# Spreading one kernel's dense matmuls anew over its attention units, and a different bank for the first product of its tail

## Chip, cores, metric

The kernel runs on one core of a Trainium2 chip. The metric is the device time of one execution in microseconds (us). The kernel before takes 654.57 us (median of 3 runs, 654.51 to 654.58). In the profile, TensorE appears as PE (matmuls) and PEld (weight loads), VectorE as DVE, ScalarE as ACT, GpSimd as POOL, and SyncE, which issues the DMAs, as SP.

## The reference

The reference has two branches on the layer norm of the same input and a residual. Branch B is a two-layer MLP over the tokens. It fills the first 387 us and the change does not touch it. Branch A is attention in 4 segments of 512 tokens with 32 heads of 32, plus a memory carried from segment to segment:

```python
phi = lambda t: jnp.where(t > 0, t + 1.0, jnp.exp(t))
for s in range(N):                                     # N = 4 segments
    qs, ks, vs = q[:, :, s], k[:, :, s], v[:, :, s]
    logits = einsum('bhqd,bhkd->bhqk', qs, ks) * scale + mask
    a_dot = einsum('bhqk,bhkd->bhqd', softmax(logits), vs)
    a_mem = einsum('bhld,bhde->bhle', phi(qs), M) / (... + 1e-06)
    outs.append(g * a_mem + (1.0 - g) * a_dot)
    M = M + einsum('bhld,bhle->bhde', phi(ks), vs)     # and z likewise
return stack(outs) @ wo
...
return x + A(xn, wq, wk, wv, wo, beta) + B(xn, w1, b1, w2, b2)
```

## The kernel before

Branch A runs as 32 "units": 4 segments of 8 groups of 4 heads. In each unit PE does two kinds of work.

- The unit's own chain. The logits of the unit are computed in two or three steps ("logits"). ScalarE takes their exp (1.88 us each), GpSimd masks them (the "select"), and one unit later PE multiplies them by v in three parts ("the weighing"). VectorE then copies ("ost"), scales ("srec"), multiplies ("prod") and adds ("o_s") the result, and a transposing DMA puts it in oT.
- Dense filler. These are jobs of 8 matmuls of 512 columns that make q, k and v of later units and the output product with wo. They are cut into pieces and put between the steps of the chain, so that PE has work while the other engines follow. Each job adds up its 8 matmuls in one of the eight banks (0 to 7) that the kernel keeps for PE's results (ps_all in the profile), and another engine then copies or adds the sum out of the bank (the job's "drain").

All of it is scheduled by hand. These are the parts that matter:

```python
def dense(self, n, side=True):            # n more matmuls of the queued jobs
    while n > 0 and self.jobs:
        job = self.jobs[0]
        at, b, reads, mm, end, on_dve = job
        stops = self.stops[on_dve] if side else ()
        if b is None:                     # a new job takes bank 6 or 7, in turn
            b = job[1] = 6 + self.turn
            self.turn ^= 1
        ...
        with fw.group(reads=reads(), writes=[self.R_bank[b]]):
            for i in range(at, stop):
                mm(b, i)
        ...
        if stop == 8:
            end(b)                        # the drain of the bank
            self.jobs.popleft()
        elif self.side and stop in stops:
            self.side.popleft()()         # one of VectorE's side tasks is queued here

# drains: q_job  ScalarE copy to qT           (line 1252 in the profile)
#         k_job  VectorE copy to kT           (line 1261)
#         v_job  ScalarE copy to vA, some on VectorE   (line 1292)
#         wo_job VectorE add to fin           (line 1306)

def unit_jobs(self, u):
    jobs = [self.wo_job(*self.wo_jobs.popleft())] if 10 <= u < self.QUOTA_FROM else []
    m = u // 4 + 1
    if m < 2 * N_SEG:
        jobs.append(self.v_job(m, u % 4))
    if u + 2 < N_UNIT:
        jobs.append(self.q_job(u + 2))
        if u + 2 < N_UNIT // 2:
            jobs.append(self.k_job(u + 2))
        ...
    if u >= self.QUOTA_FROM:              # 18: from here a unit gets a quota
        quota = self.QUOTA[u % 2] if u + 1 < N_UNIT else 100
        quota -= 8 * len(jobs) + sum(8 - j[0] for j in self.jobs)
        while quota > 0 and self.wo_jobs:
            jobs.append(self.wo_job(*self.wo_jobs.popleft()))
            quota -= 8
        self.left = max(-quota, 0)        # carried into the next unit
    return jobs

# one unit, in the order in which PE gets its work
    cuts = self.cut(total, (0, 4, 2, 4, 1, 13, 8) if even else (7, 3, 2, 4, 1, 15))
    self.dense(cuts[0]);  self.logits(u, 0)
    self.dense(cuts[1]);  self.weigh(u - 1, 0)         # bank 4
    self.dense(cuts[2], False);  self.weigh(u - 1, 1)  # bank 5
    self.dense(cuts[3], False);  self.weigh(u - 1, 2)  # bank 4 again
    # queue the side tasks for VectorE: srec; phi of q; prod; o_s; phi of k
    self.dense(cuts[4]);  self.logits(u, 1)
    if even:
        self.dense(cuts[5]);  self.logits(u, 2)
    self.dense(...)                                    # the rest of the unit's share

# the logits of all steps use banks 0 to 3; each step ends so:
    fw.op("act", exp of the four banks into pT)        # line 1363, 1.88 us
    fw.op("pool", affine_select of pT)                 # line 1367
    self.late_exps()                                   # exp of q and k for phi, line 1218

# tail: the last 8 products of 8 matmuls; product n goes to bank
    (0, 1, 2, 3, 6, 7, 5, 4)[n]
```

A dense job can start only when the job two before it has been drained from its bank. And the drain is queued on ScalarE or VectorE at the moment at which the job's last matmul is issued, so the point of the unit at which a job ends decides which work lies ahead of its drain.

## Time and profile before

| | before |
|---|---|
| time, median of 3 runs | 654.57 us |
| span of the profiled run | 652.2 us |
| PE busy | 646.7 us, 99% |
| VectorE, ScalarE, GpSimd busy | 67%, 43%, 24% |
| matmuls | 4611 |

The page of the kernel before: its first line, the first line of the busy times (each engine with its share of the span and its instructions), and the chain that ended last.

```profile
span 652.2 us, 11204 instructions
...
PE 646.7 (99%) x4611; PEld 303.1 (46%) x4611; DVE 439.9 (67%) x829; ACT 281.5 (43%) x305; POOL 154.9 (24%) x181
...
PE 90%; DVE 4%; DMA 2%; ACT 1%; POOL 1%; issue 1%; DVEq 0%
```

PE is the bound almost everywhere (busy 646.7 of 652.2 us). In the trace two dense matmuls in a row start 216 ns apart. I take that pace as given. So only stalls in PE's stream can be won.

The next view gives busy time per stretch for units 10 and 11 together and for units 14 and 15 together. The columns are the stretch in us, its length, then busy time and instructions of each engine, granted clock, DMA share, and GB/s.

```profile
core 0: us, PE busy (x) PEld busy (x) DVE busy (x) ACT busy (x) POOL busy (x), PEclk, DMA share, GB/s
461.77:481.01 19.24, 19.11 (x193) 9.35 (x194) 17.35 (x35) 13.42 (x14) 7.46 (x10) 1.00 0.51 121
...
499.94:515.61 15.67, 15.65 (x178) 7.75 (x178) 14.81 (x32) 12.45 (x11) 6.70 (x9) 1.00 0.55 138
```

VectorE is busy 17.35 of 19.24 us and 14.81 of 15.67 us there, so these units have little of VectorE to spare.

The last view of the kernel before is the timeline, at unit 28 and in the tail. Its columns are start in us, duration (with "x" more than one instruction), engine, line, operation, output<-input, shapes and count. In brackets stand the idle time of the engine just before, and what ended it.

```profile
604.73 1.22 DVE L1460 TENSOR_TENSOR prod<-ost,srec 128x1024 bf16<-128x1024 bf16 x1
...
605.10 2.11 POOL L1367 TENSOR_SCALAR_AFFINE_SELECT pT<-pT 128x512 bf16<-128x512 bf16 x2 [2.54 <-ACT pT L1363]
...
605.50 0.82 PE L199 MATMUL ps_all<-wo,oT 128*128 128x512 bf16 x3
...
606.58 0.25 PE L199 MATMUL ps_all<-vA,pT 128*128 128x33 bf16 x4 [0.26 <-POOL pT L1367]
...
607.56 0.64 POOL L1367 TENSOR_SCALAR_AFFINE_SELECT pT<-pT 128x512 bf16<-128x512 bf16 x1 [0.35 <-ACT pT L1363]
...
633.89 2.75 PE L199 MATMUL ps_all<-wo,oT 128*128 128x512 bf16 x12 [0.24 <-ACT pT L1363]
...
640.46 1.84 PEld L199 LDWEIGHTS ps_all<-wo,oT 128*128 128x128 bf16 x10 [0.49 <-DMA oT<-o_s]
```

At 606.58 the weighing waits 0.26 us for a select. The two selects that start at 605.10 take 2.11 us together, against 0.64 us for the single one at 607.56. At 633.89 the first tail product waits 0.24 us, because its bank 0 is still being read by an exp. At 640.46 a weight load waits for the transposing DMA of oT. (The idle times in brackets count from the modelled end of the last matmul. The delay against the usual distance from start to start is some 0.16 us longer: 0.42 us for this weighing, 0.41 us for this product.)

### The profile page before, as it was taken

Reading aid. Unit: us, or ns where it says so; the run is one execution under the profiler, and the core shown is the slowest. Engines: PE = TensorE matmul, PEld = TensorE weight load, DVE = VectorE, ACT = ScalarE, POOL = GpSimd, SP = SyncE. Lnnn points to the kernel's source line nnn. Section 1 sums busy time; section 2 is a strip of 40 time slices with the busy share of each in tenths; the row PEclk is TensorE's granted clock in tenths of the full one; section 3 lists DMA queues with packets and bytes.
Section 4 is the critical chain, followed back from the end, with each engine's and each line's share of the span. In section 5 each row is a group of like instructions: output and inputs, shape, how many; then the busy total and the mean of one; then the engine's idle time right before and its main releaser. Section 6 shows DMA issues by size and latency. Waiting matters only on the chain.

```text
span 652.2 us, 11204 instructions
## 1 busy us (share of the span) xinstructions
PE 646.7 (99%) x4611; PEld 303.1 (46%) x4611; DVE 439.9 (67%) x829; ACT 281.5 (43%) x305; POOL 154.9 (24%) x181
## 2 busy tenths in 40 slices
PE   9999999999999999999999999999999999999998
PEld 3444444444444444444444444444545444454444
DVE  6975775665655673745637325767898988887895
ACT  7542232232210000111101047778767788888760
POOL 2500000000011220120201203434333445544450
PEclk9999999999999999999999999999999999999999
DMA  8804242242498937629263956979644576355424
GB/s 300 217 0 130 65 116 79 65 124 70 129 265 216 231 96 210 171 87 258 66 193 116 257 136 156 190 182 227 124 120 109 152 164 144 90 115 123 114 81 138
DMA packets 190123, 95.00 MB, mean 146 GB/s; under 512 B 108664, under 2 KB 176248, under 8 KB 190072
## 3 DMA queue, kind: packets, MB, share of 16 engines
q1 hardware_dynamic: 189928, 94.25, 56.9%
q8 instruction: 36, 0.59, 0.4%
q14 instruction: 15, 0.12, 0.1%
q10 hardware_dynamic: 144, 0.03, 0.0%
HBM read 69.23 MB, written 11.53 MB: 124 GB/s over the span
## 4 chain that ended last, share of the span: by engine, by line
PE 90%; DVE 4%; DMA 2%; ACT 1%; POOL 1%; issue 1%; DVEq 0%
PE ps_all L199 90%; ACT pT L1363 1%; DMA w2s<-in_B_w_dram 1%; POOL pT L1367 1%; DVE fin L1617 1%; DVE ln_st L590 1%; DVE sum L651 0%; DVE prod L1460 0%; DMA xin<-in_A_x_dram 0%; DVE h L630 0%; POOL ln_rs L614 0%; DVE mtmp L1229 0%; DVE mtmp L1227 0%; DVE ost L1414 0%; DVE part L692 0%
## 5 line engine op out<-in xcount | busy, mean ns | idle before, releaser
L1363 ACT ACTIVATE pT<-ps_all 128x2048 bf16<-128x2048 f32 x80 | 150.2, 1877 | 47.2 <-PE ps_all L199 46.8
L1367 POOL TENSOR_SCALAR_AFFINE_SELECT pT<-pT 128x512 bf16<-128x512 bf16 x128 | 106.3, 847 | 160.9 <-ACT pT L1363 160.9
L692 DVE TENSOR_TENSOR part<-ps_all,part 128x512 f32<-128x512 f32 x84 | 57.7, 690 | 108.9 <-PE ps_all L199 88.2
L1078 POOL TENSOR_TENSOR part<-part,stg 128x512 f32<-128x512 f32 x24 | 33.0, 1402 | 285.0 <-DVE part L692 268.1
L749 ACT ACTIVATE g<-part,b1c 128x512 f16<-128x512 f32 x36 | 26.0, 722 | 99.0 <-DVE part L692 99.0
L199 PE MATMUL ps_all<-wv,xnT 128*128 128x512 bf16 x256 | 68.2, 380 | 0.2
L199 PE MATMUL ps_all<-xnT,wq 128*128 128x512 bf16 x256 | 65.6, 380 | 0.0
L199 PE MATMUL ps_all<-wo,oT 128*128 128x512 bf16 (+2 forms) x272 | 64.3, 367 | 0.2 <-ACT pT L1363 0.2
L1414 DVE CAST ost<-ps_all 128x396 bf16<-128x396 f32 (+2 forms) x96 | 44.3, 473 | 27.3 <-PE ps_all L199 26.6
L697 ACT ACTIVATE part<-ps_all 128x512 f32<-128x512 f32 x24 | 14.0, 596 | 101.4 <-PE ps_all L199 67.1
L199 PEld LDWEIGHTS ps_all<-vA,pT 128*128 128x128 bf16 x1280 | 45.5, 96 | 21.5 <-DVE ost L1414 3.3
L199 PE MATMUL ps_all<-g,sum 128*128 128x512 f16 x224 | 51.0, 379 | 0.0
L199 PE MATMUL ps_all<-g,w2s 128*128 128x512 f16 x224 | 51.0, 379 | 0.0
L199 PE MATMUL ps_all<-gT,sum 128*128 128x512 f16 x224 | 50.3, 379 | 0.1
L199 PE MATMUL ps_all<-vA,pT 128*128 128x33 bf16 x1280 | 48.5, 178 | 0.7 <-POOL pT L1367 0.6
L199 PE MATMUL ps_all<-h,sum 128*128 128x512 f16 x192 | 45.2, 379 | 0.0
L199 PE MATMUL ps_all<-h,w1s 128*128 128x512 f16 x192 | 44.9, 379 | 0.0
L199 PE MATMUL ps_all<-hT,sum 128*128 128x512 f16 x192 | 43.6, 379 | 0.0
L199 PEld LDWEIGHTS ps_all<-wo,oT 128*128 128x128 bf16 x272 | 23.8, 97 | 27.1 <-issue 4.9
L1460 DVE TENSOR_TENSOR prod<-ost,srec 128x1024 bf16<-128x1024 bf16 x24 | 35.1, 1461 | 0.0
L199 PEld LDWEIGHTS ps_all<-gT,sum 128*128 128x128 f16 x224 | 21.8, 98 | 26.8 <-DVE gT L666 0.6
L199 PEld LDWEIGHTS ps_all<-g,w2s 128*128 128x128 bf16 x224 | 21.9, 98 | 26.4
(118 smaller groups left out, 862.2 us busy)
## 6 DMA issues: line engine op xcount, KB each, us to landing
w2s<-in_B_w_dram SPq DMA_DIRECT2D x8, 1792.0 KB, 9.5
w1s<-in_B_w_dram SPq DMA_DIRECT2D x12, 1024.0 KB, 5.6
wq<-in_A_wq_dram SPq DMA_DIRECT2D x32, 256.0 KB, 3.4
xs<-in_A_x_dram SPq DMA_DIRECT2D x24, 256.0 KB, 3.4
stg<-in_A_x_dram SPq DMA_DIRECT2D x16, 256.0 KB, 2.8
out_dram<-stg SPq DMA_DIRECT2D x16, 256.0 KB, 3.8
wk<-in_A_wk_dram SPq DMA_DIRECT2D x16, 256.0 KB, 3.4
fin<-out_dram SPq DMA_DIRECT2D x16, 256.0 KB, 3.3
```

Source lines behind the costliest of these rows:

```text
L199: ins = self.nc.tensor.matmul(*args, **kwargs)
L590: fw.op("dve", lambda e: e.bn_stats(st[:, 6 * h:6 * h + 6], src[:, 512 * h:512 * h + 512]), reads=[self.R_xin[c]], writes=[R])
L692: self.fw.op("dve", lambda e: e.tensor_tensor(self.tmp[dst][:], self.bank(b), self.tmp[src][:], op=ALU.add), reads=[self.R_bank[b], self.R ...
L697: self.fw.op("act", lambda e: e.activation(self.tmp[dst][:], self.bank(b), ACT.Copy), reads=[self.R_bank[b]], writes=[self.R_tmp[dst]])
L749: self.fw.op("act", lambda e: e.activation(self.gB[f % 2][half][:, f // 2, :], src, ACT.Gelu_apprx_tanh, bias=self.b1c[:, f:f + 1], scale= ...
L1078: fw.op("pool", lambda e: e.tensor_tensor(self.tmp[t][:], self.tmp[t][:], self.stg[k][:, 512 * half:512 * half + 512], op=ALU.add), reads= ...
L1363: fw.op("act", lambda e: e.activation(dst, src, ACT.Exp, scale=SCALE), reads=self.R_bank[0:4], writes=[R[v % 2][kb] for v, kb, _ in blocks ...
L1367: fw.op("pool", lambda e: e.affine_select(d, d, pattern=[[0, 4], [1, P]], compare_op=ALU.is_ge, fill=0.0, base=0, channel_multiplier=-1), ...
L1414: fw.op("dve", lambda e: e.tensor_copy(dst, src), reads=[self.R_bank[b]], writes=[self.R_ost[o][part]])
L1460: fw.op("dve", lambda e: e.tensor_tensor(self.prod[:], ost[:, :, 0:D_HEAD], rec.unsqueeze(2).to_broadcast([P, 32, D_HEAD]), op=ALU.mult), ...
L1617: fw.op("dve", lambda e: e.tensor_tensor(dst, self.ps[:, b, c0:c1], dst.bitcast(F16), op=ALU.add), reads=[self.R_bank[b], R], writes=[R])
```

## The change

The change evens out the units. From unit 10 on it gives each unit a quota of matmuls, 30 and 26 in turn in units 10 to 13, then 25 and 21. In the even units with few matmuls it puts one more dense matmul ahead of the weighing. In the tail it gives the first product the dense bank that is idle, and it moves two matmuls of product 5 behind the last steps of the others.

```diff
--- before.py
+++ after.py
@@ -1486,14 +1486,13 @@
         fw.op("act", lambda e: e.activation(self.oT[s % 3][:, g, :], bb, ACT.Copy),
               reads=[self.R_bank[b]], writes=[self.R_oT[s % 3][g]])
 
-    QUOTA_FROM, QUOTA = 18, (24, 20)
+    WO_FROM, QUOTA = 10, ((30, 26), (25, 21))
     STOPS = ((1, 4, 7), (1, 4))
     STOPS_FEW = ((1, 3, 5, 7), (1, 3, 5))
     XN_AT = (0, 1, 2, 3, 6, 7, 8, 9, 14, 15, 16, 17)
 
     def unit_jobs(self, u):
-        jobs = [self.wo_job(*self.wo_jobs.popleft())] if 10 <= u < self.QUOTA_FROM else []
-        m = u // 4 + 1
+        jobs, m = [], u // 4 + 1
         if m < 2 * N_SEG:
             jobs.append(self.v_job(m, u % 4))
         if u + 2 < N_UNIT:
@@ -1502,8 +1501,8 @@
                 jobs.append(self.k_job(u + 2))
             else:
                 self.k_load(u + 2)
-        if u >= self.QUOTA_FROM:
-            quota = self.QUOTA[u % 2] if u + 1 < N_UNIT else 100
+        if u >= self.WO_FROM:
+            quota = self.QUOTA[u >= 14][u % 2] if u + 1 < N_UNIT else 100
             quota -= 8 * len(jobs) + sum(8 - j[0] for j in self.jobs)
             while quota > 0 and self.wo_jobs:
                 jobs.append(self.wo_job(*self.wo_jobs.popleft()))
@@ -1544,7 +1543,9 @@
             if u in self.XN_AT[::4]:
                 self.xn_load(xn)
                 self.xn_load(xn + 1)
-            if u < 10 or u >= 14 and total <= 26:
+            if u >= 14 and total <= 26:
+                cuts = self.cut(total, (0, 5, 2, 4, 1, 12, 8) if even else (7, 3, 2, 4, 1, 15))
+            elif u < 10:
                 cuts = self.cut(total, (0, 4, 2, 4, 1, 13, 8) if even else (7, 3, 2, 4, 1, 15))
             else:
                 cuts = self.cut(total, (0, 4, 2, 2, 2, 14, 8) if even else (7, 3, 2, 2, 2, 16))
@@ -1603,7 +1604,7 @@
         fw.wait_outputs(3)
 
         def product(n, j0, j1, cols=((0, 512),)):
-            i, h, b = n // 2, n % 2, (0, 1, 2, 3, 6, 7, 5, 4)[n]
+            i, h, b = n // 2, n % 2, (6 + self.turn, 0, 1, 2, 3, 7 - self.turn, 5, 4)[n]
             for p, (c0, c1) in enumerate(cols):
                 with fw.group(reads=self.R_wo[j0:j1] + self.R_oT[s % 3][j0:j1], writes=[self.R_bank[b]]):
                     for jc in range(j0, j1):
@@ -1634,9 +1635,10 @@
         product(4, 0, 7)
         self.o_transpose(u, 4)
         product(3, 6, 7)
-        product(5, 0, 7)
-        for n in range(6):
+        product(5, 0, 5)
+        for n in range(5):
             product(n, 7, 8)
+        product(5, 5, 8)
         product(6, 0, 8)
         product(7, 0, 8, ((0, 256), (256, 384), (384, 512)))
 
```

By the order of the instructions, units 10 to 13 go from 39 and 25 dense matmuls (even, odd) to 36 and 20, units 14 to 17 from 29 and 19 to 30 and 16, even units from 18 on from 28 to 30, and the last stretch from 92 to 98. The number of matmuls stays at 4611.

## The prediction

> **What bounds it now.** The page shows PE busy 646.7 of 652.2 us (99%); the chain of waits is 90% PE. In the timeline, dense 512-column matmuls start every 216 ns[...]. Both kernels issue the same 4611 matmuls, so only stalls inside that stream can be won. From start-to-start gaps after 387 us:
>
> - Even units, last dense matmul to first weighing product, waiting for the POOL select: 0.21, 0.21, 0.09, 0.09, 0.35, 0.42, 0.35 us in units 16, 18, 20, 24, 26, 28, 30: 1.7 us.
> - Odd units from 19 on, first logits of the next unit waiting for the exp that still reads banks 0 to 3: 0.09 us x 6: 0.55 us.
> - Dense matmul after the first logits in units 22, 26, 30: 0.16, 0.07, 0.07 us.
> - Unit 11: 0.31 us, unit 15: 0.18 us; VectorE drains late there.
> - Tail: 0.41 us at 633.9 (first product in bank 0 waits for the exp), 0.16 us at 640.5 (transpose DMA of unit 30), about 0.15 us at the end, where VectorE's ten final adds run back to back from 645.00.
>
> Sum about 3.8 us: 0.6%.
>
> **What the change moves.** By the instruction order, units 10 to 13 go from 39/25 dense matmuls to 36/20, units 14 to 17 from 29/19 to 30/16, even units from 18 on from 28 to 30 (odd ones stay at 16), the last stretch from 92 to 98. Even units get 4 instead of 3 dense matmuls before the weighing, and 10 instead of 9 lie between an odd unit's second logits and the next unit: 0.43 us more cover for the select, 0.22 us for the exp. That removes the exp waits and nearly all select waits (about 0.08 us stays in 26, 28, 30): about 2.2 us. The first tail product in the idle dense bank removes 0.41 us; the extra matmuls cover the transpose (0.16); moving two matmuls of product 5 later starts the final adds 0.4 us sooner; 0.15 count. Gain: 2.5 to 3 us.
>
> **What it costs.** VectorE. In units 10 and 11 it is busy 17.3 of 19.2 us (busy time by window); the pair shrinks to about 17.2 us of PE work and VectorE to about 16.6 (one 0.68 us add fewer): 96%. In 14 and 15 it is busy 14.8 of 15.7; the pair shrinks to about 15. Odd units have 3 instead of 4 dense matmuls between weighing parts 0 and 2, which share a bank. So I expect stalls of 0.2 to 0.5 us in units 11 and 15, perhaps 13 and 17, in all 0.3 to 1 us more than before's 0.5.
>
> **Prediction.** 652.4 us, range 651.3 to 654.1. Faster by over 2%: 0.01; within 2%: 0.98; slower by over 2%: 0.01.
>
> **What would show it.** Right: even units from 16 on wait under 0.1 us before the weighing; no gap before the odd-to-even logits; no 0.4 us gap at the first tail product; last add bound by PE. New PE gaps, if any, lie in units 10 to 17, before weighing part 2 or a dense matmul, ended by VectorE.
>
> **What would make it wrong.** VectorE's backlog in units 10 to 17 costing over 2 us and lasting; bank waits in even units; selects slowed by VectorE's products shifting into them (the select took 1.35 us there, 0.63 us alone).

## The result, and the profile after

The changed kernel takes 660.17 us (median of 6 runs, 658.8 to 660.9), against 654.56 us (654.23 to 654.83) for the kernel before in the same rounds. The ratio is 1.0085 (95% interval 1.0072 to 1.0098). Here and below a ratio is the mean time of one kernel's fast runs over that of the other's of the same rounds, so it is not quite the ratio of the medians quoted. The outputs are correct. The change is 0.85% slower. That is inside the 2% band, but well outside the predicted range of 651.3 to 654.1 us, and on the other side of zero.

Five of the six runs had a mean granted clock of 0.997. The sixth, which is the profiled one, had 1.0 and took 658.8 us. At full clock the loss is therefore 4.2 us, and the rest comes in the runs with the lower clock.

The page of the changed kernel (51 of its matmul records are missing; the program has 4611):

```profile
span 657.1 us, 11144 instructions
...
PE 641.0 (98%) x4560; PEld 303.4 (46%) x4611; DVE 440.7 (67%) x829; ACT 281.2 (43%) x305; POOL 151.0 (23%) x181
...
PE 89%; DVE 5%; ACT 3%; issue 2%; DMA 0%; POOL 0%
```

The chain now names VectorE with 5% and ScalarE with 3%, against 4% and 1%. The list of what PE waited for says which instructions of theirs. The columns are the total in us, how often, and the longest wait. First the kernel before:

```profile
PE ps_all L199 <- POOL pT L1367: 0.6, 3, 0.3
PE ps_all L199 <- ACT pT L1363: 0.4, 2, 0.2
```

And the changed kernel:

```profile
PE ps_all L199 <- issue: 2.2, 14, 0.2
PE ps_all L199 <- ACT vA L1292: 1.9, 2, 0.9
PE ps_all L199 <- DVE fin L1306: 1.7, 1, 1.7
...
PE ps_all L199 <- ACT qT L1252: 0.8, 2, 0.4
PE ps_all L199 <- DMA oT<-o_s: 0.8, 1, 0.8
PE ps_all L199 <- DVE ost L1414: 0.7, 3, 0.3
PE ps_all L199 <- DVE kT L1261: 0.6, 1, 0.6
PE ps_all L199 <- POOL pT L1367: 0.3, 1, 0.3
```

In the kernel before, this list had only GpSimd's selects (0.6 us), an exp (0.4 us) and one wait early in the MLP (1.3 us, and the same after). The drains of v, wo, q and k, the ost copy and the DMA are all new in it (it leaves out the shortest waits). The 14 entries called "issue" are no stalls but holes left by missing matmul records: t_queue below, with the same order on PE and a complete trace, has no such entry.

The busy times of the same pairs of units:

```profile
461.69:479.24 17.55, 17.11 (x183) 8.57 (x186) 15.89 (x33) 13.42 (x14) 7.20 (x9) 1.00 0.55 111
...
497.25:514.65 17.40, 15.01 (x172) 7.68 (x174) 15.25 (x33) 12.18 (x11) 6.05 (x9) 1.00 0.57 139
```

The work of units 14 and 15 shrank as predicted (PE is busy 15.01 us), but they take 17.40 us instead of 15.67 us. The timeline of unit 15 shows where the pair loses most:

```profile
506.76 0.74 DVE L1466 TENSOR_TENSOR o_s<-prod 128x512 bf16<-128x512 bf16 x1
...
507.42 0.72 DVE L1227 TENSOR_SCALAR mtmp<-etmp 128x512 bf16<-128x512 bf16 x1
...
508.17 0.69 DVE L1229 SCALAR_TENSOR_TENSOR mtmp<-kT,mtmp 128x512 bf16<-128x512 bf16 x1
508.78 0.68 DVE L1306 TENSOR_TENSOR fin<-ps_all,fin 128x512 bf16<-128x512 f32 x1
...
509.52 0.39 PE L199 MATMUL ps_all<-wv,xnT 128*128 128x512 bf16 x1 [1.73 <-DVE fin L1306]
```

A job of v needs the bank that an output product has left. The product's drain ("fin", 508.78) comes on VectorE after o_s, and after the two steps of phi of k (lines 1227 and 1229). PE waits 1.73 us.

In unit 16 the queue that PE waits for is ScalarE's:

```profile
518.84 0.39 PE L199 MATMUL ps_all<-wv,xnT 128*128 128x512 bf16 x1
...
518.96 1.88 ACT L1363 ACTIVATE pT<-ps_all 128x2048 bf16<-128x2048 f32 x1 [1.49 <-PE ps_all L199]
...
520.73 0.62 ACT L1218 ACTIVATE etmp<-qT 128x512 bf16<-128x512 bf16 x1
...
521.25 0.59 ACT L1292 ACTIVATE vA<-ps_all 128x512 bf16<-128x512 f32 x1
...
521.90 0.39 PE L199 MATMUL ps_all<-wo,oT 128*128 128x512 bf16 x1 [0.94 <-ACT vA L1292]
```

The last matmul of the v job ends just after the logits, so its drain (521.25) stands in ScalarE's queue behind the 1.88 us exp of these logits and a small exp. The output product that wants the bank starts at 521.90.

In the tail the products' steps that use the oT of unit 30 wait for its DMA:

```profile
640.00 1.22 DVE L1460 TENSOR_TENSOR prod<-ost,srec 128x1024 bf16<-128x1024 bf16 x1
...
641.14 0.69 DVE L1306 TENSOR_TENSOR fin<-ps_all,fin 128x512 bf16<-128x512 f32 x1
...
641.74 0.41 DVE L1466 TENSOR_TENSOR o_s<-prod 128x512 bf16<-128x512 bf16 x1
...
642.73 1.20 SPq L221 DMA_TRANSPOSE oT<-o_s  x1
...
645.70 2.33 PE L199 MATMUL ps_all<-wo,oT 128*128 128x512 bf16 x10 [0.80 <-DMA oT<-o_s]
```

The o_s of unit 30 is done only at 642.15, and its transpose holds PE back until 645.70. In the kernel before, the same prod started 2.4 us after the second logits of unit 31, in which it runs (633.84 against 631.41). Here it starts 4.4 us after them (640.00 against 635.60). A fin add (636.78) is queued ahead of srec, and the later srec and phi steps then run beside a select: 0.66 and 0.77 us for two of them, where the kernel before had 0.19 and 0.28. A second fin add (641.14) stands ahead of o_s, as one did in the kernel before.

The next table has the stall of each unit: the time from a unit's first logits to the next unit's, less what the same order of instructions takes at the usual start-to-start distances (216 ns between two dense matmuls, and so on for each pair of kinds, read from the trace). Values of a few hundredths, also negative ones, are scatter. The last row counts all units from 10 on, also those left out above it. The last four columns belong to experiments described below (unit 15 of t_ahead contains a stretch at half clock).

| unit, stall in us | before | after | t_ahead | t_queue | t_all | c_odd_even |
|---|---|---|---|---|---|---|
| 11 | 0.35 | 0.39 | 0.39 | 0.39 | 0.38 | 0.35 |
| 12 | -0.02 | 0.79 | 0.79 | -0.02 | -0.02 | -0.02 |
| 15 | 0.23 | 2.40 | 3.82 | 0.58 | 0.58 | 0.23 |
| 16 | 0.20 | 1.10 | -0.02 | 1.68 | 0.74 | 0.20 |
| 17 | 0.04 | 0.04 | 0.65 | 0.04 | 0.43 | 0.04 |
| 18 | 0.21 | 0.95 | 0.35 | 0.94 | 0.35 | 0.21 |
| 20 | 0.08 | 0.45 | 0.44 | 0.45 | 0.45 | 0.15 |
| 24 | 0.08 | 1.10 | -0.02 | 1.10 | -0.02 | 0.16 |
| 26 | 0.40 | 0.66 | 0.06 | 0.65 | 0.06 | 0.28 |
| 28 | 0.40 | 0.04 | 0.04 | 0.04 | 0.04 | 0.27 |
| 30 | 0.43 | 0.05 | 0.05 | 0.05 | 0.06 | 0.31 |
| 31, to the last matmul | 0.62 | 1.02 | 1.13 | 1.10 | 0.05 | 0.05 |
| sum of 10 to 31 | 3.95 | 9.27 | 7.97 | 7.31 | 3.37 | 2.62 |

The stalls grew by 5.3 us. The end after the last matmul got 0.4 us shorter (2.90 to 2.51 us), and unit 10 started 0.1 us earlier. That makes 4.8 us, which is the difference of the spans, 657.1 and 652.2, to within rounding.

### The profile page after: what moved, and what is told of

It reads as the page before. It is cut to its first block, busy times and chain, and to the rows that moved or that the text cites. A ratio compares the mean times of both kernels' runs of the same rounds, so it can differ in the third digit from the quotient of the medians.

```text
span 657.1 us, 11144 instructions
## 1 busy us (share of the span) xinstructions
PE 641.0 (98%) x4560; PEld 303.4 (46%) x4611; DVE 440.7 (67%) x829; ACT 281.2 (43%) x305; POOL 151.0 (23%) x181
## 4 chain that ended last, share of the span: by engine, by line
PE 89%; DVE 5%; ACT 3%; issue 2%; DMA 0%; POOL 0%
PE ps_all L199 89%; ACT pT L1363 2%; DVE prod L1460 1%; DVE mtmp L1227 1%; DVE fin L1306 1%; DVE ost L1414 1%; DMA oT<-o_s 0%; DVE mtmp L1229 0%; ACT vA L1292 0%; DVE o_s L1466 0%; DVE srec L1456 0%; DVE srec L1457 0%; POOL pT L1367 0%; ACT etmp L1218 0%; DVE kT L1261 0%
## 5 line engine op out<-in xcount | busy, mean ns | idle before, releaser
L1367 POOL TENSOR_SCALAR_AFFINE_SELECT pT<-pT 128x512 bf16<-128x512 bf16 x128 | 102.3, 817 | 168.1 <-ACT pT L1363 168.0
L199 PE MATMUL ps_all<-wv,xnT 128*128 128x512 bf16 x239 | 65.5, 380 | 4.0 <-DVE fin L1306 1.7
L199 PE MATMUL ps_all<-wo,oT 128*128 128x512 bf16 (+2 forms) x259 | 60.0, 366 | 4.0 <-ACT vA L1292 1.9
L199 PE MATMUL ps_all<-xnT,wq 128*128 128x512 bf16 x242 | 62.4, 380 | 0.4 <-issue 0.2
L199 PEld LDWEIGHTS ps_all<-g,sum 128*128 128x128 f16 x224 | 21.9, 98 | 26.4 <-DVE part L692 0.2
```

The costliest lines, as they stand in the source:

```text
L199: ins = self.nc.tensor.matmul(*args, **kwargs)
L1367: fw.op("pool", lambda e: e.affine_select(d, d, pattern=[[0, 4], [1, P]], compare_op=ALU.is_ge, fill=0.0, base=0, channel_multiplier=-1), ...
```

## The experiments

The theory after the result was this. The quotas lose time because they move the points at which jobs end, so that drains fall behind long work in ScalarE's and VectorE's queues. The rivals were that VectorE simply has too much to do in units 10 to 17, so that a backlog lasts; that the extra matmul ahead of the weighing or the tail costs something; and that the chip's clock does it. All twelve runs gave correct outputs. Each was timed in rounds beside the kernel before.

### e_tail: the tail's edit alone

```diff
-            i, h, b = n // 2, n % 2, (0, 1, 2, 3, 6, 7, 5, 4)[n]
+            i, h, b = n // 2, n % 2, (6 + self.turn, 0, 1, 2, 3, 7 - self.turn, 5, 4)[n]
...
-        product(5, 0, 7)
-        for n in range(6):
+        product(5, 0, 5)
+        for n in range(5):
             product(n, 7, 8)
+        product(5, 5, 8)
```

> Kernel before with only the tail of the change (first tail product in the idle dense bank, two matmuls of product 5 later). If the tail part is sound by itself: the 0.41 us gap ahead of the first product in bank 0 goes and the last adds are no longer back to back, 0.5 to 0.6 us less, about 654.0 us. If the tail part is what costs (it carries a new 0.9 us gap in the changed kernel): 655 us or more.

It took 653.75 us (653.31 to 653.97), against 654.31 us for the kernel before; ratio 0.999 (0.9975 to 1.0005). The stall of the last unit fell from 0.62 to 0.37 us, and VectorE now waits 0.16 us for PE before its last add, where the ten adds had run back to back. The span of the profiled run is 0.6 us shorter (651.6 against 652.2 us). The interval reaches 1, so the times alone don't prove a gain, but the tail's edit is not what lost the time.

### e_cuts: the one matmul more ahead of the weighing, alone

```diff
-            if u < 10 or u >= 14 and total <= 26:
+            if u >= 14 and total <= 26:
+                cuts = self.cut(total, (0, 5, 2, 4, 1, 12, 8) if even else (7, 3, 2, 4, 1, 15))
+            elif u < 10:
```

> Kernel before with only the new cut (one more dense matmul ahead of the weighing in even units from 14 on). My reading: each of the waits for the POOL select in units 16 to 30 shrinks by up to 0.22 us, in all 1.0 to 1.3 us less, about 653.4 us, and no new gap. If moving that matmul is what loses time in the changed kernel: 655 us or more.

It took 655.09 us (654.93 to 655.16); ratio 1.0011 (0.9996 to 1.0026). Units 26, 28 and 30 gained 0.21 us each, as the extra cover should give. But units 20 and 24 lost 0.6 us each and unit 15 lost 0.2 us. The cut leaves one matmul fewer between the parts of the weighing, and a fin add falls ahead of the ost copy that frees bank 4 for part 2. So the reading in the expectation was wrong: alone, this cut costs some 0.8 us in the trace (the interval reaches 1). In the changed kernel, where the quotas give even units more matmuls, four and not three stay between these parts, and units 20 and 24 have no such wait for ost.

### e_quota: the quotas alone

```diff
-    QUOTA_FROM, QUOTA = 18, (24, 20)
+    WO_FROM, QUOTA = 10, ((30, 26), (25, 21))
...
-        jobs = [self.wo_job(*self.wo_jobs.popleft())] if 10 <= u < self.QUOTA_FROM else []
-        m = u // 4 + 1
+        jobs, m = [], u // 4 + 1
...
-        if u >= self.QUOTA_FROM:
-            quota = self.QUOTA[u % 2] if u + 1 < N_UNIT else 100
+        if u >= self.WO_FROM:
+            quota = self.QUOTA[u >= 14][u % 2] if u + 1 < N_UNIT else 100
```

> Kernel before with only the new quotas from unit 10 on; old cuts, old tail. My theory: the quotas decide which dense job ends where, and through that all new gaps come: 659 to 662 us, with gaps of about 1 us in units 16 and 24 and 0.6 us in 18 and 26 ended by ScalarE's drains, and over 1.5 us in unit 15 ended by VectorE. If the parts only lose in combination: under 657 us.

It took 660.47 us (659.35 to 662.06); ratio 1.01 (1.0081 to 1.012). Two runs at a clock of 1.0 took 659.35 and 659.7 us, two at 0.997 took 661.23 and 662.06 us. The stalls in units 12, 15, 16 and 24 (0.79, 2.12, 1.10 and 1.10 us) are those of the whole change or close to them (0.79, 2.40, 1.10 and 1.10 us). The quotas alone bring the whole loss.

### e_from14: the change, but units 10 to 13 as before

```diff
-    QUOTA_FROM, QUOTA = 18, (24, 20)
+    QUOTA_FROM, QUOTA = 14, (25, 21)
...
```

(The cuts and the tail are those of the changed kernel.)

> Changed kernel, but units 10 to 13 keep the work of before (64 dense matmuls a pair and not 56); units 14 to 29 have exactly the changed kernel's order on the tensor engine. If VectorE's backlog built up in units 10 to 13 is the whole cause (my prediction's cost): all gaps of units 11 to 18 go and the time is 653.5 us or less. If the cause is local to each unit (which job ends just ahead of an exp): gaps of 1.1 us in 16 and 24 and 0.6 us in 18 and 26 stay as they are, only 11, 12 and part of unit 15 shrink: 655.5 to 658 us.

It took 657.84 us (657.78 to 658.35); ratio 1.0055 (1.004 to 1.007), with a clock of 1.0 in all four runs. Unit 12's stall was gone (-0.02 us) and unit 15's fell from 2.40 to 1.26 us. Units 16 and 24 kept their 1.10 us. So about half of unit 15's stall came with the shorter units ahead of it (a backlog). The other half, and all of ScalarE's waits, did not. Units 30 and 31 stalled 0.8 us more than in the changed kernel, so the time fell by less than units 12 and 15 gained.

### t_ahead: the changed kernel with ScalarE's drains ahead of the exp

In units 16 and 24 one matmul more goes ahead of the second logits, and in units 18 and 26 one more ahead of the third. The drain of the job that ends there then gets in front of the exp.

```diff
+            if u in (16, 18, 24, 26):
+                cuts[3 if u % 8 == 0 else 5] += 1
+                cuts[6] -= 1
```

> Changed kernel with one or two dense matmuls moved across a logits group in four units, so that the v product of units 16 and 24 ends ahead of the second logits and the q product of units 18 and 26 ahead of the third; their ScalarE drains are then queued ahead of the 1.88 us exp and not behind it. If a drain behind an exp makes the gaps: the 1.1 us gaps in 16 and 24 and the 0.59 us gaps in 18 and 26 fall under 0.3 us each, about 2.5 to 3.3 us less than the changed kernel, 657 to 657.7 us. If they come from something else that lasts (too few dense matmuls in the odd units, VectorE): they stay or move to a neighbouring unit, 659.5 us or more.

It took 657.52 us (655.89 to 657.89), against 654.3 us for the kernel before; ratio 1.0042 (1.0027 to 1.0057). The one run at a clock of 1.0 took 655.89 us, 2.9 us less than the changed kernel's run at that clock. The timeline of unit 16 shows the new order:

```profile
519.93 0.60 ACT L1292 ACTIVATE vA<-ps_all 128x512 bf16<-128x512 f32 x1 [0.67 <-PE ps_all L199]
...
520.97 1.88 ACT L1363 ACTIVATE pT<-ps_all 128x2048 bf16<-128x2048 f32 x1 [0.44 <-PE ps_all L199]
...
522.59 0.59 PE L199 MATMUL ps_all<-wo,oT 128*128 128x512 bf16 x2
```

The drain of v now starts at 519.93, ahead of the exp at 520.97, and the output product at 522.59 waits for nothing. The stalls of units 16 and 24 went from 1.10 us to -0.02, of 18 from 0.95 to 0.35 and of 26 from 0.66 to 0.06. Unit 17 took 0.6 us back. One matmul per unit in another place removed 3.4 us of waits, with the same work on every engine. That is queue order, not load.

The run also caught the clock in the act. Unit 15's idle stretch is followed by a stretch at half clock (windows view, columns as above; the clock is the 1.00 or 0.50 near the end of the line):

```profile
508.10:510.00 1.90, 0.17 (x5) 0.10 (x2) 1.87 (x4) 1.12 (x1) 0.91 (x2) 1.00 0.34 69
511.50:514.90 3.40, 3.40 (x34) 1.65 (x35) 2.47 (x9) 1.27 (x1) 0.00 (x0) 0.50 0.84 213
514.90:520.00 5.10, 5.10 (x60) 2.65 (x59) 3.38 (x5) 3.53 (x5) 2.72 (x3) 1.00 0.54 120
```

PE was busy 0.17 us of the 1.90 us from 508.10. From 511.5 to 514.9 its granted clock was 0.50. Unit 15 lost 1.4 us more than in the profile of the changed kernel.

### t_queue: the changed kernel with another order of VectorE's queue

PE's order stays the same to the instruction. In unit 12 no side task is queued on VectorE during the k job, and in unit 14 none during the output products, so the drain that the next job needs comes first.

```diff
-        return [0, None, ..., mm, finish, ring is self.wk_ring]          # q and k jobs
+        return [0, None, ..., mm, finish, 2 * (ring is self.wk_ring)]
...
-        return [0, None, ..., mm, end, True]                             # wo jobs
+        return [0, None, ..., mm, end, 3]
...
+            self.stops += (() if u == 12 else self.stops[1], () if u == 14 else self.stops[1])
```

> Changed kernel with the same instructions in the same order on the tensor engine; only VectorE's queue is ordered otherwise in units 12 and 14: the k drain goes ahead of the product and add of the combine, and the output add of a wo product ahead of them and of phi. If place in VectorE's queue makes the gaps: 0.8 us in unit 12 goes and the 1.9 us in unit 15 falls under 0.7 us, 1.5 to 2.5 us less than the changed kernel, 657.7 to 658.7 us. If VectorE is simply short of time there (its backlog): the waits move into units 13, 15, 16 and the sum of the stalls of units 11 to 17 stays within 0.5 us of 4.8 us.

It took 657.1 us (656.95 to 657.33); ratio 1.0041 (1.0026 to 1.0056), with a clock of 1.0 in all runs; that is somewhat better than expected. Unit 12's stall was gone and unit 15's fell from 2.40 to 0.58 us. Unit 16 got 0.58 us more, so part of the delay had only moved. The timeline of units 14 and 15:

```profile
505.03 0.68 DVE L1306 TENSOR_TENSOR fin<-ps_all,fin 128x512 bf16<-128x512 f32 x1
...
505.63 1.22 DVE L1460 TENSOR_TENSOR prod<-ost,srec 128x1024 bf16<-128x1024 bf16 x1
...
507.17 0.38 PE L199 MATMUL ps_all<-wv,xnT 128*128 128x512 bf16 x1
```

The fin add (505.03) is now ahead of prod (505.63), and the v matmul at 507.17 starts without idle time. Against the changed kernel's run at full clock this saves 1.7 us. With the same load on VectorE and the same PE order, 2.0 us of stalls went. Nor did the clock fall in any of the four runs (1.0 in each), with the long idle stretch gone.

### h_long and h_short: does an idle stretch lower the clock?

Both put holds into early units of a kernel that is the one before in all else. PE waits for selects on a tile that nobody uses yet, three in a row for h_long (before units 3, 5 and 7) and one for h_short (twice in each of units 3 to 7).

```diff
+    def hold(self, n):
+        fw, t, R = self.fw, self.oT[1][:, 0, :], self.R_oT[1][0]
+        pe = fw.E["pe"]
+        tok = _Tok("pe", pe.sem, pe.n)
+        ...
+        for _ in range(n):
+            tok = fw.op("pool", lambda e: e.affine_select(t, t, ...), reads=[R], writes=[R], extra=[tok])
+        pe.wait_tok(tok)
...
+            if u in (3, 5, 7):        # h_short: if 3 <= u <= 7, here and once more in the unit
+                self.hold(3)          # h_short: self.hold(1)
```

> Kernel before with three deliberate holds of the tensor engine, in units 3, 5 and 7: each waits for three POOL selects on a spare tile in a chain after its last matmul (0.64 us each), about 2 us. If an idle stretch of that length can halve the granted clock for 3.4 us (as in the changed kernel's runs at clock 0.997): some of its runs show a mean clock under 1.0 and take about 1.5 us more per dip than 6 us of holds, 661 to 665 us in all. If idle stretches do nothing to the clock: 1.0 in all runs and about 660.5 us.

> As h_long, but ten holds of one select each (about 0.8 us) in units 3 to 7: more idle time in sum, in short pieces. If it is the length of one idle stretch that counts: clock 1.0 in all runs, 661 to 663 us. If it is idle time in sum: dips here too.

The holds came out longer than planned, because a memset of 0.53 us and real selects stood ahead of them in GpSimd's queue. h_long took 666.49 us (666.12 to 669.37; ratio 1.0192, 1.0171 to 1.0213) and h_short 668.55 us (667.07 to 668.71; ratio 1.0206, 1.0189 to 1.0223), against 654.57 us. In h_long PE stood idle 3.37, 2.79 and 2.79 us. In the profiled run three stretches have a granted clock of 0.50, one with each hold: 412.70 to 419.50, 433.20 to 440.00 and 453.70 to 457.10 us (6.8, 6.8 and 3.4 us). All four runs had a mean clock of 0.987 to 0.995. In h_short the ten stretches were 1.97, 0.98, 1.38, 0.76, 1.38, 0.98, 1.38, 0.76, 1.38 and 0.98 us. The windows view of its first hold and what came after:

```profile
410.30:412.20 1.90, 0.00 (x0) 0.00 (x0) 0.00 (x0) 0.00 (x0) 1.83 (x4) 1.00 0.79 178
413.10:416.50 3.40, 3.40 (x49) 2.04 (x48) 1.33 (x3) 2.00 (x2) 0.63 (x1) 0.50 0.87 202
416.60:420.00 3.40, 2.42 (x20) 1.05 (x19) 2.92 (x8) 1.81 (x2) 0.63 (x1) 1.00 0.01 5
```

Only the first stretch, 1.97 us, was followed by a half clock (0.50 from 413.10 to 416.50), and three of four runs had a mean of 0.997. After the nine of 0.76 to 1.38 us there was none. Both texts had planned for other lengths, so these two runs don't test their numbers as written. What they do show is that the total of idle time did not decide here: h_short has the longer total (11.9 us in the holds against 8.9), but one stretch at half clock in its profile against three. And one single stretch of 1.97 us was followed by 3.4 us at a clock of 0.50.

### c_odd and c_odd_even: the kernel before with the aims of the change, reached by other moves

Both start from e_tail. c_odd moves the second logits of odd units from 19 on one piece earlier. That puts more matmuls behind them, which covers the exp that the next unit waits for.

```diff
+            if u > 18 and not even and u + 1 < N_UNIT:
+                cuts[5] += cuts[4]
+                cuts[4] = 0
```

> Kernel before with the change's tail, and in odd units from 19 on the one dense matmul ahead of the second logits moved behind them: 10 and not 9 lie between these logits and the next unit's. If the exp waits of 0.09 us and part of the select waits of units 26, 28, 30 are covered by that: 0.55 + 0.6 us under the tail alone, about 652.6 us. If the gain is lost to later drains as in the change: 653.7 us or more.

It took 653.49 us (653.27 to 653.55); ratio 0.9985 (0.997 to 1.0). The exp waits went, but the select waits of units 26, 28 and 30 rose from 0.40 to 0.50 us. So it gained 0.3 us over e_tail where I had expected 1.15. In the trace the first select ended 0.50 us after VectorE's prod (606.20 and 605.70). Prod does not depend on these logits, so earlier logits do not bring the select forward.

c_odd_even adds one matmul ahead of the weighing in units 26, 28 and 30 only, and in the tail it puts six steps of product 4 ahead of the steps that wait for the transpose.

```diff
+            if u >= 26 and even:
+                cuts[1] += 1
+                cuts[3] -= 1
...
-        for n in range(3):
+        product(4, 0, 6)
+        for n in (0, 1, 2, 4):
             product(n, 6, 7)
-        product(4, 0, 7)
```

> As c_odd, and in units 26, 28, 30 one dense matmul more ahead of the weighing (taken from between parts 1 and 2), and in the tail the first six steps of product 4 go ahead of the steps that need the transposed unit 30. The select waits left in 26, 28, 30 (about 0.15 us each) and the wait of 0.3 us for the transposing DMA go: 0.5 to 0.8 us under c_odd, about 652.0 us. If the weighing drains come late for it, as they did in units 20 and 24 when the cut was moved there: no gain over c_odd.

It took 652.58 us (652.44 to 652.87); ratio 0.9973 (0.9956 to 0.9989). This is the lowest time, under that of the kernel before and of the changed one. (The ratio of t_all below lies within its interval.) The stall of the last unit is 0.05 us, and 26, 28 and 30 have 0.28, 0.27 and 0.31 us left.

### t_all: the whole change with its order put right

This is the changed kernel with t_ahead, t_queue and the tail order of c_odd_even.

```diff
+            if u in (16, 18, 24, 26):
+                cuts[3 if u % 8 == 0 else 5] += 1
+                cuts[6] -= 1
+            self.stops += (() if u == 12 else self.stops[1], () if u == 14 else self.stops[1])
...
-        for n in range(3):
+        product(4, 0, 6)
+        for n in (0, 1, 2, 4):
             product(n, 6, 7)
-        product(4, 0, 7)
```

(And the two edits of job classes shown for t_queue.)

> Changed kernel with three corrections together, each of which alters order only: the ends of the v and q products ahead of the logits (t_ahead), VectorE's queue in units 12 and 14 (t_queue), and the first six steps of tail product 4 ahead of those that need the transposed unit 30. If places in the queues of the draining engines and the tail's transpose are the whole loss: stalls from unit 10 on of 3.0 to 4.3 us, no clock dip, 653.7 to 655.0 us, that is, level with the kernel before. If the quotas themselves leave VectorE short of time: 655.5 us or more.

It took 652.94 us (652.83 to 653.06); ratio 0.9975 (0.996 to 0.999), better than expected. The change's quotas, cuts and tail are all in it, and its stalls sum to 3.37 us, against 9.27. So most of the loss is not the quotas or VectorE's load but the order that the quotas happened to give. Two things limit this. Units 11 to 17 still stall 1.3 us more in sum than in the kernel before. And the new tail order is an improvement in its own right: the last unit stalls 0.05 us, against 0.62 us in the kernel before. c_odd_even has this tail with the old quotas and took 652.58 us, so no run shows that the quotas themselves gain anything.

### c_first: prod ahead of phi of q on VectorE

This is c_odd_even with VectorE's prod queued ahead of phi of q in odd units from 19 on, because the select seemed to wait for prod.

```diff
+            if u > 18 and not even:
+                self.side.append(steps.pop(0))
```

> c_odd_even with VectorE's product of the combine ahead of phi of q in odd units from 19 on, so that it ends before the POOL select starts. If POOL waits for that product: the select of units 25, 27, 29 falls from 1.56 us to under 0.9 us, the gaps of 0.14 us ahead of the weighing in 26, 28, 30 go, and the time is 0.3 to 0.5 us under c_odd_even, about 652.2 us. If the select is slow by itself: no change.

It took 657.07 us (656.94 to 657.15); ratio 1.0038 (1.0023 to 1.0053), 4.5 us slower than c_odd_even where I had expected a gain. The timeline of unit 28:

```profile
607.05 1.23 DVE L1460 TENSOR_TENSOR prod<-ost,srec 128x1024 bf16<-128x1024 bf16 x1
...
608.02 1.39 POOL L1367 TENSOR_SCALAR_AFFINE_SELECT pT<-pT 128x512 bf16<-128x512 bf16 x2 [2.33 <-ACT pT L1363]
608.19 0.72 DVE L1227 TENSOR_SCALAR mtmp<-etmp 128x512 bf16<-128x512 bf16 x1
...
608.95 1.00 DVE L1229 SCALAR_TENSOR_TENSOR pqT<-qT,mtmp 128x512 bf16<-128x512 bf16 x1
...
610.00 0.27 PE L199 MATMUL ps_all<-vA,pT 128*128 128x33 bf16 x4 [0.42 <-DVE pqT L1229]
```

The first half of the expectation held. The two selects (608.02) take 1.39 us, against 2.33 us in c_odd_even and 2.11 us before. But now it is the two steps of phi of q (mtmp and pqT) that meet them: 0.72 us instead of 0.28 for mtmp, and 1.00 us instead of 0.69 for pqT. The weighing needs pqT, so PE waits for it, at 610.00. The stalls of units 20, 22 and 24 rose to 1.2 us each and those of 26, 28 and 30 to about 0.6 us.

The traces show selects and prods taking longer where they overlap, whichever started first. A select took 0.63 us alone and prod 1.22 us. In the kernel before, each of the 22 selects that start during a prod ended 0.49 to 0.50 us after that prod's end and took 1.34 to 1.69 us, and each of the 13 prods that start during a select took 1.65 to 1.68 us. (A select that did nothing at all until prod's end would end 0.63 us after it, so these selects did not stand quite still during the prod.) Why was not shown.

## Why the prediction was wrong, and where it was right

**The step that failed first: "So I expect stalls of 0.2 to 0.5 us in units 11 and 15, perhaps 13 and 17, in all 0.3 to 1 us more than before's 0.5."** VectorE's stalls measured 0.33 us in unit 11, 0.81 in unit 12, and 1.9 (the wait for fin, start to start) and 0.45 in unit 15. That is about 3.5 us, so 3 us more than before. The mechanism named was right, and the places nearly so. The size was not. I had put down the cost from the share of busy time in a stretch, and that share came out lower than I had said (15.89 of 17.55 us in units 10 and 11, 91% and not 96%). But a wait depends on what stands ahead of one drain at one moment: prod, o_s and phi of k, up to 2 us of it. t_queue shows this, with the same load, another order, and 2.0 us less. e_from14 shows that load had a share too, about half of unit 15.

**A term that was missing: ScalarE.** The cost part began and ended with "VectorE". ScalarE is busy 43% of the time, so I did not follow its queue. Four jobs now end right behind a logits step, and their drains queue behind an exp of 1.88 us: 1.11 us in units 16 and 24 and 0.59 us in 18 and 26, 3.4 us together. This is the largest single part of the loss, and t_ahead removed it with one matmul per unit. The trace of unit 16 shows the order: the drain at 521.25 started behind both exps that were queued ahead of it (518.96 and 520.73), 0.1 us before the end of the second. "Bank waits in even units" was named as a risk, and it is what came. But it had no place in the sum or in the range.

**A second missing term: the clock.** Five of the six runs of the changed kernel had a mean clock of 0.997, and their median is 1.6 us above the time of the sixth, which had 1.0. In the profile of t_ahead the clock was 0.50 from 511.50 to 514.90, after unit 15's idle stretch (PE busy 0.17 of the 1.90 us from 508.10). In h_short one idle stretch of 1.97 us was followed by 0.50, while nine of 0.76 to 1.38 us were not. Not every run with the long stretch has a lower clock: 5 of 6, 2 of 4 in e_quota, 3 of 4 in t_ahead and in h_short. In the profiled run of the changed kernel PE stood idle for the 1.73 us from 507.79, and the clock was 1.00 from 505.20 to 520.00; e_quota's profiled run is the same (busy 0.03 of the 1.50 us from 508.00, clock 1.0). What decides whether the clock falls was not shown; that unit 15's stretch brought the fall in the unprofiled runs too is my estimate, from their mean of 0.997, which is also the mean of t_ahead's profiled run.

**"The extra matmuls cover the transpose (0.16)": wrong in its sign.** The wait for the DMA of oT became 0.96 us. The quotas leave another piece of an output product behind the second logits of unit 31, so a job ends early there and its fin add is queued ahead of the srec and prod of unit 30's result; prod starts 2 us later after the logits than before. That the tail can be had without this wait is shown by t_all and c_odd_even, whose last unit stalls 0.05 us.

**The list of select waits was partly misread.** In units 16, 18, 20 and 24 the wait before the weighing's last part was for the ost copy that frees bank 4 (it ended 54 to 58 ns before the matmul in the trace), not for the select. Only 26, 28 and 30, with 0.35, 0.42 and 0.35 us, were select waits. So of the 1.7 us listed only 1.1 could be won by one matmul more ahead of the weighing. In e_cuts that matmul made the ost waits of 20 and 24 worse, by 0.6 us each.

**What held.** The 216 ns pace and the equal number of matmuls held. The exp waits at the start of even units went (0.09 us, six times). The selects of 26, 28 and 30 fell to 0.09, 0.07 and 0.08 us. The first gap of the tail (0.41 us) went, and the end after the last matmul became shorter. The new VectorE gaps lay in units 11, 12 and 15, inside the stretch named. The gains came about in the size foreseen. The new waits sum to some 8 us (ScalarE's drains 3.4, units 12, 15 and 18 on VectorE 3.3, a select in unit 20 0.5, the DMA in the tail 0.8). The span grew by 4.8 us, so by difference some 3 us were gained, which is what the prediction had put there (2.5 to 3). The match is partly luck: the ost waits of units 16, 20 and 24 (0.21, 0.09 and 0.09 us) went as well, but not through the cover that the prediction named, since they were no select waits.

## What to carry to other kernels

When filler work is moved between fixed steps, follow each drain and not the busy share: for every job, ask which instruction stands ahead of its drain in that engine's queue at the place where the job now ends, and which later job needs its buffer. If a rebalancing loses time, try to put its drains back in front with one or two moved instructions before giving up the balance; here that turned a loss of 0.85% into a gain of 0.25%. Then ask whether the balance is needed: c_odd_even, without it, did as well. Count a wait of nearly 2 us on PE at more than its length: here the clock was 0.50 for 3.4 us after one of 1.97 us (h_short) and after one of 1.73 us (t_ahead), though not after every one.
